# Seven-product gate/up blocks built inside PSUM, in a four-stage pipeline, with sums for the down stages on GpSimd

## The chip, the cores and the metric

One core of one Trainium2 chip. The metric is the device time of one execution in microseconds, as the median of several executions on the chip. Every execution lists its span by the profiler and the mean granted TensorE clock. All executions used here were of the fast state (the chip has a second, slower one) at a granted clock of 0.996 to 1.0. The time of an execution is longer than its span, and not by the same amount for both kernels: by 1.67 to 1.79 us in the 33 listed executions of the kernel before, by 1.77 to 3.14 us (median 2.15) in the 11 of the changed one. So spans are compared with spans and medians with medians.

## The reference, cut to what matters

Two blocks read the same 2048 x 640 input: a linear attention with 32 heads, and a GeGLU feed-forward with 1728 inner columns. A sigmoid gate mixes them. Inputs and output are bf16.

```python
q, k, v = split_heads(x @ wqkv)                   # 32 heads of 20
pq, pk = phi(q), phi(k)                           # phi(t) = where(t > 0, t + 1, exp(t)) + 1e-6
num = einsum("bhqd,bhde->bhqe", pq, einsum("bhsd,bhse->bhde", pk, v))
den = einsum("bhqd,bhd->bhq", pq, pk.sum over s)[..., None] + 1e-6
a = merge_heads(num / den) @ wo
b = (gelu(x @ w_gate) * (x @ w_up)) @ w_down
out = g * a + (1 - g) * b                         # g = sigmoid((x * gate_w).sum(-1))
```

## The kernel before

The 2048 rows are 16 positions of 128, in four row blocks (`q`) of 512. A row block has a **gate/up stage** (13 units of 128 inner columns, each `x @ w_gate` and `x @ w_up`, and one half unit) and a **down stage**. TensorE works through row block 0's gate/up, the K and G matrices of all positions, then gate/up 1, down 0, gate/up 2, down 1, gate/up 3, down 2, down 3.

A plain unit is ten matmuls of 512 columns. A **block** does the same by Strassen's scheme: it takes gate and up as the two rows of a 2 x 2 block matrix product and needs seven products of half the width in place of eight. For that it needs sums of weights (`ws`, later fetched from DRAM into `wr`) and of tokens (`tx`). The block before collects its parts in SBUF (`cg`, `ut`), and GpSimd makes the last product:

```python
    def phase_EW(q, ft, early, fetch):
        # ... x, ub, gb are PSUM banks, cg and ut SBUF tiles
        ew_mm(x[:, lo_h], 2, s_(2), t_(2), False, True)
        nc.scalar.copy(out=cg[:, hi_h], in_=x[:, lo_h])
        # ... four more products
        nc.vector.tensor_tensor(out=cg[:, hi_h], in0=ub[:, hi_h], in1=cg[:, hi_h], op=ALU.add)
        nc.scalar.activation(out=ut[:, 1], in_=x[:, lo_h], func=ACT.Copy, scale=HS)
        w_fetch(*fetch, eng=dma2)
        # ...
        nc.vector.tensor_tensor(out=cg, in0=gb, in1=cg, op=ALU.add)
        nc.vector.scalar_tensor_tensor(out=ut[:], in0=ub..., scalar=HS, in1=ut[:, 1:2]..., op0=ALU.mult, op1=ALU.add)
        # later: gelu on ScalarE, and hT = ut * gelu on GpSimd
```

The denominators of the attention are made for two positions at a time. GpSimd multiplies, VectorE reduces and inverts, GpSimd scales, and a transposing transfer brings the result into `pqT`.

```python
    def den_inv(st):
        for i in range(2):
            nc.vector.tensor_reduce(out=den[:, i, :], in_=dn[st + i]...)          # den <- prod
        nc.vector.scalar_tensor_tensor(out=dtmp[:], in0=den[:], scalar=EPS,       # two SBUF inputs
                                       in1=gsc["en"]..., op0=ALU.add, op1=ALU.mult)
        nc.vector.reciprocal(out=rg..., in_=dtmp[:])
```

The list `side` says which of this work is issued at which step of which stage. The down stages are Strassen products too; they need the **S sums** (`phase_S`, tiles `sw`, `s`, `sp`), which in this kernel VectorE makes, spread over the steps of the next gate/up stage.

Of the kernel before, what the change touches and what calls it, by code (L numbers as in the profile page):

```python
# [16 lines left out]
def kernel(  # L17
# [12 lines left out]
    nc = tc.nc  # L30
# [29 lines left out]
    def sums(out, a0, a1, op):  # L60
        nc.vector.tensor_tensor(out=out, in0=a0, in1=a1, op=op)
# [11 lines left out]
    held = set()  # L73

    def ps_tile(name, hold=False):
        b = bank_at[0] % NB
        while b in held:
            b = (b + 1) % NB
        bank_at[0] = b + 1
        if hold:  # L80
            held.add(b)
        return banks[:, b * QW : (b + 1) * QW]
# [8 lines left out]
    WF = tuple(range(4, 11))  # L91
    WS = 2 * 4 + 1
# [25 lines left out]
    def x_tiles():  # L118
        tx = big.tile([P, 4, 2, HT], FP16, name="tx", tag="pq", bufs=NQ)
        ew["tx"] = [tx[:, n] for n in range(4)]  # L120

    def cg_tile():
        ew["cg"] = big.tile([P, 2, QW], FP32, name="cg", tag="pq", bufs=NQ)

    x_tiles()
    cg_tile()
# [10 lines left out]

    ident = consts.tile([P, P], BF16, name="ident")
# [83 lines left out]
    def e_out(q, ft, psg, psu):  # L222
        gl = work.tile([P, QW], BF16, name="gl")
        nc.scalar.activation(out=gl[:], in_=psg[:], func=ACT.Gelu_apprx_tanh)  # L224
        nc.vector.scalar_tensor_tensor(out=hT_cur[q][:, ft, :], in0=psu[:], scalar=HS, in1=gl[:],  # L225
                                       op0=ALU.mult, op1=ALU.mult)

    def phase_E(q, ft, early=None):
        if ft < NF - 1:
            psg = ps_tile("ps_g")  # L230
            e_mm(psg, wg, ft, q)
            if early:
                early()
                ew_finish()
            psu = ps_tile("ps_u")
            e_mm(psu, wu, ft, q)
            e_out(q, ft, psg, psu)
        else:
            pgu = ps_tile("ps_gu")
            e_mm(pgu, wgu, 0, q)  # L240
            if early:
                early()
                ew_finish()
            gl = work.tile([P, QW], BF16, name="gl")
            nc.scalar.activation(out=gl[0:FL, :], in_=pgu[0:FL, :], func=ACT.Gelu_apprx_tanh)
            nc.vector.scalar_tensor_tensor(out=hT_cur[q][0:FL, ft, :], in0=pgu[FL:P, :], scalar=HS,
                                           in1=gl[0:FL, :], op0=ALU.mult, op1=ALU.mult)

    stash = dram.tile([len(WF), P, WS, P], FP16, name="stash")

    def w_sums(i):
        n = len(WF[2 * i : 2 * i + 2])
# [4 lines left out]
        for out, a0, a1, op in ((s1, u[:, :, 0:2, :], u[:, :, 2:4, :], ALU.add), (s2, s1, g[:, :, 0:2, :], ALU.subtract),  # L257
                                (s3, g[:, :, 0:2, :], u[:, :, 0:2, :], ALU.subtract),
                                (s4, g[:, :, 2:4, :], s2, ALU.subtract),
                                (o[:, 0:n, 8:9, :], g[:, :, 4:5, :], u[:, :, 4:5, :], ALU.subtract)):  # L260
# [18 lines left out]
    def ew_tiles():  # L279
        cg = ew["cg"]  # L280
        ew["cg"] = [cg[:, 0], cg[:, 1], zacc[:, 0:QW]]
        ew["n"] = 2
        ew["first"] = {}
        ew["open"] = []
        ew.setdefault("at", {})

    def w_fetch(*keys, eng=dma):
# [4 lines left out]
        for q, ft in keys:  # L292
            slot = ew["ring"][ew["m"] % 2]
            ew["m"] += 1
            eng(out=slot, in_=stash[WF.index(ft)])
            ew["at"][q, ft] = slot

    def ew_finish():
        for f in ew.get("open", ()):
            f()  # L300
        ew["open"] = []

    lo_h, hi_h = slice(0, HT), slice(HT, QW)

    def ew_mm(out, k, lhs, rhs, start=False, stop=False):
        for n in range(k):
            nc.tensor.matmul(out, lhsT=lhs(n), rhs=rhs(n), start=start and n == 0, stop=stop and n == k - 1,  # L307
                             skip_group_check=True)

    def ew_first(q, ft):  # L310
        x = ps_tile("ps_wx")
        cg = ew["cg"][ew["n"] % 3]
        ew["n"] += 1
        ew_mm(x[:, lo_h], 2, lambda n: wg[:, n, ft * P : (ft + 1) * P], lambda n: xT[q][:, n, lo_h], True, True)
        nc.scalar.copy(out=cg[:, lo_h], in_=x[:, lo_h])
        ew["first"][q, ft] = x, cg

    def phase_EW(q, ft, early, fetch):
        fs = slice(ft * P, (ft + 1) * P)
        sw_ = ew["at"][q, ft]  # L320
        if (q, ft) not in ew["first"]:
            ew_first(q, ft)
        x, cg = ew["first"][q, ft]

        def wt(w, k0):
            return lambda n: w[:, k0 + n, fs]

        def xt(k0, c):
            return lambda n: xT[q][:, k0 + n, c]

        def s_(i):
            return lambda n: sw_[:, 2 * (i - 1) + n, :]

        def t_(i):
            return lambda n: ew["tx"][i - 1][:, n, :]

        ub, gb = ps_tile("ps_wu"), ps_tile("ps_wg")
        ew_mm(ub, 1, wt(wu, 4), xt(4, slice(0, QW)), True)
        ew_mm(ub[:, lo_h], 2, wt(wu, 2), t_(4))
        ew_mm(gb[:, lo_h], 1, wt(wg, 4), xt(4, lo_h), True)  # L340
        ew_mm(gb[:, hi_h], 1, s_(5), xt(4, hi_h))
        ew_mm(x[:, lo_h], 2, s_(2), t_(2), False, True)
        nc.scalar.copy(out=cg[:, hi_h], in_=x[:, lo_h])
        early()
        ew_mm(gb[:, lo_h], 2, wt(wg, 2), xt(2, lo_h))
        ew_mm(ub[:, hi_h], 2, s_(1), t_(1), False, True)
        ew_mm(gb[:, hi_h], 2, s_(4), xt(2, hi_h), False, True)
        ew_mm(x[:, lo_h], 2, s_(3), t_(3), False, True)
        ut = work.tile([P, 2, HT], FP32, name="ut", tag="prod", bufs=2)
        nc.vector.tensor_tensor(out=cg[:, hi_h], in0=ub[:, hi_h], in1=cg[:, hi_h], op=ALU.add)  # L350
        nc.scalar.activation(out=ut[:, 1], in_=x[:, lo_h], func=ACT.Copy, scale=HS)  # L351
        w_fetch(*fetch, eng=dma2)
        ew_finish()
        nc.vector.tensor_tensor(out=cg, in0=gb, in1=cg, op=ALU.add)
        nc.vector.scalar_tensor_tensor(out=ut[:], in0=ub.rearrange("p (j c) -> p j c", j=2), scalar=HS,  # L355
                                       in1=ut[:, 1:2].to_broadcast([P, 2, HT]), op0=ALU.mult, op1=ALU.add)

        def finish():
            gl = work.tile([P, QW], BF16, name="gl")
            nc.scalar.activation(out=gl[:], in_=cg, func=ACT.Gelu_apprx_tanh)  # L360
            nc.gpsimd.tensor_tensor(out=hT_cur[q][:, ft, :], in0=ut[:].rearrange("p j c -> p (j c)"), in1=gl[:],  # L361
                                    op=ALU.mult)

        ew["open"].append(finish)
# [49 lines left out]
    def phase_KQ3(st):  # L414
# [3 lines left out]
        for lo, hi in CF:  # L418
            for dk in range(ND):
                kq_mm(ps[:, lo:hi], st, dk, lo, hi)  # L420
            top = min(hi, WQK - 1)
# [135 lines left out]
    zacc = consts.tile([P, D], FP32, name="zacc")  # L557
# [111 lines left out]
    def den_inv(st):  # L669
        den = work.tile([P, 2, H], FP32, name="den", bufs=2)  # L670
        for i in range(2):
            nc.vector.tensor_reduce(out=den[:, i, :], in_=dn[st + i][:].rearrange("p (h c) -> p h c", c=Dh),  # L672
                                    axis=AX.X, op=ALU.add)
        dtmp = work.tile([P, 2, H], FP32, name="dtmp", bufs=2)
        nc.vector.scalar_tensor_tensor(
            out=dtmp[:], in0=den[:], scalar=EPS, in1=gsc["en"][:, st : st + 2, None].to_broadcast([P, 2, H]),
# [4 lines left out]
        dn[st], dn[st + 1] = rg[:, 0], rg[:, 1]  # L681

# [36 lines left out]
    def phase_S(q, part, a=None, which=(3, 1, 2, 4)):  # L719
# [3 lines left out]
        def blk(i, k):  # L723
            return ktiles(part, k, hT_cur[q], pqT[q])[:, :, i * TW + c0 : i * TW + c1]

        s = {i: SS[q, i][:, lo:hi, c0:c1] for i in range(1, 5)}
        for i in which:
            a0, a1, op = {3: (blk(0, 0), blk(1, 0), ALU.subtract), 1: (blk(1, 0), blk(1, 1), ALU.add),
                          2: (s[1], blk(0, 0), ALU.subtract), 4: (blk(0, 1), s[2], ALU.subtract)}[i]
            sums(s[i], a0, a1, op)  # L730
# [12 lines left out]
    def phase_F(q):  # L743
# [34 lines left out]
        for a in range(2):  # L778
# [19 lines left out]
            product(x, a, 0, 0, 0, 0, 0, 0, True, True)  # L798
            c1 = keep("c1", x, 0)
# [32 lines left out]

    runs = {
        0: [3, -4, -5, 12, 13, -6, -7, 10, -8, 9, 11],
        1: list(range(1, NF)),
        2: [13, 0, 1, -4, -5, 2, -6, -7, 3, -8, -9, 12, -10, 11],
        3: [13, 0, 1, 2, -4, -5, 3, -6, -7, 12, -8, -9, 10, 11],
    }
    wins = [(q, -ft) for q in runs if q > 1 for ft in runs[q] if ft < 0]

    def next_fetch(q, ft):
        if (q, ft) not in wins:
            return ()
        k = wins.index((q, ft)) + 2
        return wins[k : k + 1]

    def run_E(q):
        for n, ft in enumerate(runs[q]):
            nxt = runs[q][n + 1] if n + 1 < len(runs[q]) else 0
            early = (lambda f=-nxt: ew_first(q, f)) if nxt < 0 else (lambda: None)  # L850
            if ft < 0:
                phase_EW(q, -ft, early, next_fetch(q, -ft))
            else:
                phase_E(q, ft, early if q != 1 else None)
            beside(q, n + (q == 1))
        ew_finish()

    with tc.manual_schedule(engines={mybir.EngineType.PE, mybir.EngineType.Activation, mybir.EngineType.DVE}):
# [9 lines left out]
    ew_tiles()  # L868
    side.update({
        (0, 0): [(w_sums, 1)],  # L870
        (0, 2): [(w_sums, 2)],
        (0, 8): [(x_sums, 3)],
# [3 lines left out]
    with tc.manual_schedule():  # L876
# [3 lines left out]
        w_sums(3)  # L880
# [25 lines left out]
    phase_E(1, 0)  # L906
    phase_KV()
    phase_Zrep()
# [20 lines left out]
    def m_part(i):  # L929
        phase_M(((0, 0), (0, 1), (1, 0)) if i == 0 else ((1, 1), (2, 0), (2, 1)))  # L930

    side.update({
        ("C", 0, 0): [(h_twin, 1)],
# [69 lines left out]
```

## Time and profile before

| | before |
|---|---|
| median of the runs given at the start (6) | 263.04 us |
| median of the 20 runs given with the result, these 6 among them | 262.23 us |
| median in the later sessions | 262.1 to 262.6 us |
| profiled span | 260.5 us |
| TensorE busy | 98% of the span |
| start of row block 0's gate/up | 21.8 us |
| gate/up of row block 0, 1, 2, 3 | 23.96, 31.77, 27.85, 27.96 us |
| K and G | 52.06 us |
| down stages 0 and 1 | 17.87 us each |

How to read it: TensorE is the bound from 12 us on, so a change is worth what it takes off TensorE's list, less the holes that it opens there. A stage's length is the distance between the first matmuls of two stages in TensorE's timeline. Row block 1's stage has further work in it besides its units, among it the products M, which join the attention's K-V sums with `wo`. The prediction below shows the lines that this rests on.

### The profile page before, as it was taken

The numbers are of one execution on the slowest core, as the hardware profiler recorded it, in microseconds if no ns is written. First come the engines' busy times: TensorE is split into PE (matmuls) and PEld (weight loads), VectorE is DVE, ScalarE is ACT, GpSimd is POOL, SyncE is SP. The second block draws the span as 40 slices with busy tenths as digits, with TensorE's granted clock in tenths as the row PEclk, the third lists the DMA queues.
The fourth block names the chain that finished last, engine by engine and source line by source line (L and its number), as shares of the span: only waits on it lengthen the run. The fifth ranks groups of instructions, "written<-read, shape, count | busy, mean of one in ns | idle before, by whom it ended". The sixth has DMA issues, their size and how long they took to land.

```text
span 260.5 us, 4715 instructions
## 1 busy us (share of the span) xinstructions
PE 255.3 (98%) x1713; PEld 156.7 (60%) x1713; DVE 203.6 (78%) x400; ACT 112.3 (43%) x241; POOL 106.4 (41%) x112
## 2 busy tenths in 40 slices
PE   7999999999999999999999999999999999999994
PEld 3554675555556775444476666757665775767672
DVE  0697667478779995699999969998789999777632
ACT  3689546655555233832231146654113665312110
POOL 6109896644551003685001875332892643000000
PEclk9999999999999999999999999999999999999999
DMA  6999999700000019125021258330123630011011
GB/s 222 280 300 306 205 321 276 302 4 0 0 0 3 0 21 334 42 69 112 9 93 52 50 107 150 104 113 1 53 50 101 143 92 0 3 50 47 6 50 50
DMA packets 37842, 26.84 MB, mean 103 GB/s; under 512 B 21052, under 2 KB 35260, under 8 KB 37820
## 3 DMA queue, kind: packets, MB, share of 16 engines
q1 hardware_dynamic: 35794, 22.81, 31.8%
q10 hardware_dynamic: 2026, 3.74, 5.5%
q8 instruction: 13, 0.21, 0.3%
q14 instruction: 9, 0.07, 0.1%
HBM read 16.45 MB, written 4.69 MB: 81 GB/s over the span
## 4 chain that ended last, share of the span: by engine, by line
PE 94%; DMA 4%; DVE 0%; SPq 0%; issue 0%
PE banks L219 30%; PE banks L764 26%; PE banks L405 15%; PE banks L307 14%; PE banks L503 6%; DMA wqk<-in_A_wqkv_dram 3%; PE banks L494 2%; DMA x_all<-in_A_x_dram 1%; PE banks L771 1%; PE banks L634 0%; PE banks L603 0%; DVE o_out L790 0%; SPq L155 0%; PE banks L573 0%
## 5 line engine op out<-in xcount | busy, mean ns | idle before, releaser
L224 ACT ACTIVATE gl<-banks 128x512 bf16<-128x512 f32 x34 | 20.2, 596 | 21.8 <-PE banks L219 18.6
L219 PEld LDWEIGHTS <-wu 128*128 128x128 bf16 x170 | 16.6, 98 | 18.2
L219 PEld LDWEIGHTS <-wg 128*128 128x128 bf16 x170 | 16.3, 98 | 16.9 <-issue 0.5
L422 ACT ACTIVATE phi<-banks 128x512 bf16<-128x512 f32 (+1 forms) x36 | 18.8, 526 | 16.3 <-POOL hold L737 8.9
L361 POOL TENSOR_TENSOR hT_151<-ut,gl 128x512 bf16<-128x512 f32 x12 | 15.0, 1260 | 14.6 <-ACT gl L360 11.0
L786 ACT ACTIVATE m_all<-banks,omg_s 128x320 f32<-128x320 f32 x16 | 8.4, 527 | 27.3 <-PE banks L764 27.2
L225 DVE SCALAR_TENSOR_TENSOR hb<-banks,gl 128x512 bf16<-128x512 f32 x20 | 13.4, 676 | 4.8 <-PE banks L219 2.6
L219 PE MATMUL banks<-xT_89,wg 128*128 128x512 bf16 x65 | 16.2, 379 | 0.0
L219 PE MATMUL banks<-xT_89,wu 128*128 128x512 bf16 x65 | 16.2, 379 | 0.0
L666 POOL TENSOR_TENSOR prod<-pq_95,zrep 128x640 f32<-128x640 bf16 x4 | 7.4, 1864 | 21.1 <-DVE den L672 21.1
L307 PE MATMUL banks<-tx,wr 128*128 128x256 f16 x78 | 14.9, 273 | 0.0
L790 DVE SCALAR_TENSOR_TENSOR o_out<-banks,omg_s,m_all 128x320 bf16<-128x320 f32 x24 | 12.0, 536 | 3.1 <-PE banks L764 3.1
L225 DVE SCALAR_TENSOR_TENSOR hT_151<-banks,gl 128x512 bf16<-128x512 f32 x14 | 9.6, 684 | 5.4 <-PE banks L219 2.4
L786 ACT ACTIVATE sw<-banks,omg_s 128x320 f32<-128x320 f32 x8 | 4.2, 528 | 21.0 <-PE banks L764 21.0
L405 PE MATMUL banks<-wqk,xT_88 128*128 128x512 bf16 (+2 forms) x80 | 12.3, 300 | 0.9 <-DMA wqk<-in_A_wqkv_dram 0.9
L355 DVE SCALAR_TENSOR_TENSOR ut<-banks,ut 128x512 f32<-128x512 f32 x18 | 12.3, 681 | 0.9 <-ACT ut L351 0.9
L424 DVE TENSOR_SCALAR phi<-phi 128x1280 bf16<-128x1280 bf16 x12 | 5.9, 492 | 8.8 <-ACT eneg L423 5.5
L307 PEld LDWEIGHTS <-wr 128*128 128x128 f16 x117 | 11.4, 98 | 1.5 <-DMA wr<-stash 0.2
L672 DVE TENSOR_REDUCE den<-prod 128x32 f32<-128x640 f32 x14 | 10.8, 810 | 0.9 <-POOL prod L666 0.9
L405 PE MATMUL banks<-wqk,xT_89 128*128 128x512 bf16 (+1 forms) x60 | 11.5, 344 | 0.0
L405 PE MATMUL banks<-wqk,xT_91 128*128 128x512 bf16 (+1 forms) x60 | 11.5, 344 | 0.0
L405 PE MATMUL banks<-wqk,xT_90 128*128 128x512 bf16 (+1 forms) x60 | 11.5, 344 | 0.0
(278 smaller groups left out, 645.1 us busy)
## 6 DMA issues: line engine op xcount, KB each, us to landing
wr<-stash ACTq DMA_DIRECT2D x11, 288.0 KB, 2.8
out_dram<-o_out SPq DMA_DIRECT2D x16, 160.0 KB, 1.7
wd<-in_B_w_down_dram SPq DMA_DIRECT2D x1, 2080.0 KB
x_all<-in_A_x_dram SPq DMA_DIRECT2D x3, 640.0 KB, 4.8
wqk<-in_A_wqkv_dram SPq DMA_DIRECT2D x1, 800.0 KB
wg<-in_B_w_gate_dram SPq DMA_DIRECT2D x1, 800.0 KB
wu<-in_B_w_up_dram SPq DMA_DIRECT2D x1, 800.0 KB
wv<-in_A_wqkv_dram SPq DMA_DIRECT2D x1, 800.0 KB
```

The costliest lines, as they stand in the source:

```text
L219: nc.tensor.matmul(ps[:, t0 : t0 + tw], lhsT=w[:, dk, ft * P : (ft + 1) * P], rhs=xT[q][:, dk, t0 : t0 + tw], start=(dk == 0), stop=(dk == ...
L224: nc.scalar.activation(out=gl[:], in_=psg[:], func=ACT.Gelu_apprx_tanh)
L225: nc.vector.scalar_tensor_tensor(out=hT_cur[q][:, ft, :], in0=psu[:], scalar=HS, in1=gl[:], op0=ALU.mult, op1=ALU.mult)
L307: nc.tensor.matmul(out, lhsT=lhs(n), rhs=rhs(n), start=start and n == 0, stop=stop and n == k - 1, skip_group_check=True)
L355: nc.vector.scalar_tensor_tensor(out=ut[:], in0=ub.rearrange("p (j c) -> p j c", j=2), scalar=HS, in1=ut[:, 1:2].to_broadcast([P, 2, HT]), ...
L361: nc.gpsimd.tensor_tensor(out=hT_cur[q][:, ft, :], in0=ut[:].rearrange("p j c -> p (j c)"), in1=gl[:], op=ALU.mult)
L405: nc.tensor.matmul(ps[:, 0 : hi - lo], lhsT=xT[q][:, dk, sl * P : (sl + 1) * P], rhs=wqk[:, dk, lo:hi], start=(dk == 0), stop=(dk == ND - 1),)
L422: nc.scalar.activation(out=e[:, lo:top], in_=ps[:, lo:top], func=ACT.Exp)
L503: nc.tensor.matmul(bank[:, 0:HALF], lhsT=lhsT, rhs=rhs, start=(start and n == 0), stop=(stop and n == NG2 - 1), skip_group_check=True)
L764: nc.tensor.matmul(bank[:, 0:HALF], lhsT=lhs(sa, ia, ka * KS + kk, a), rhs=rhs(sb, kb * KS + kk, jb), start=(start and kk == 0), stop=(sto ...
L786: nc.scalar.activation(out=c[:], in_=bank[:, 0:HALF], func=ACT.Copy, scale=omg[i])
L790: nc.vector.scalar_tensor_tensor(out=out, in0=bank[:, 0:HALF], scalar=omg[i], in1=c[:], op0=ALU.mult, op1=ALU.add)
```

## The change

The intent: 28 blocks in place of 18. For that a block must need less of the other engines. It is now built inside PSUM, the memory that matmuls write to (eight banks here, `GB` and `UB` in the diff): ScalarE copies a half bank into another bank, VectorE adds into a bank, and matmuls go on adding to what they wrote. Four stages of consecutive blocks are interleaved on TensorE so that these steps lie beside other blocks' products. A plain unit ("filler") is put beside the first two steps, when the pipeline is not yet full (the **ramp**; the steps that empty it are the **drain**). VectorE gets `hT` back from GpSimd. GpSimd gets the S sums of row blocks 1 and 2. There are four fetch buffers in place of two, and the fetches move from ScalarE's queue to SyncE's.

```diff
+    GB, UB = (0, 1, 2), (3, 4, 5, 6, 7)
...
+        def p1():
+            two(ub[:, lo_h], wg[:, 0:2, fs], X[:, 0:2, lo_h])
+            nc.scalar.copy(out=gb[:, lo_h], in_=ub[:, lo_h])
+            nc.scalar.copy(out=cp, in_=ub[:, hi_h])
+        def p6():
+            two(ub[:, lo_h], s_(2), tx[1])
+            nc.vector.tensor_tensor(out=gb[:, hi_h], in0=ub[:, lo_h], in1=cp, op=ALU.add)
+        def p7():
+            two(ub[:, lo_h], s_(3), tx[2])
+            nc.scalar.copy(out=c3, in_=ub[:, lo_h])
+        def p3():
+            nc.vector.tensor_tensor(out=ub[:, hi_h], in0=ub[:, hi_h], in1=c3, op=ALU.add)
+            two(gb[:, hi_h], s_(4), X[:, 2:4, hi_h])
+            w_fetch(*fetch)
...
+        return [p5, p1], [p6], [p7, p3, g5, p2], [u5, p4]
...
-        2: [13, 0, 1, -4, -5, 2, -6, -7, 3, -8, -9, 12, -10, 11],
-        3: [13, 0, 1, 2, -4, -5, 3, -6, -7, 12, -8, -9, 10, 11],
+        2: blocks([NF - 1, 1, 12], 0, range(2, 12), [None]),
+        3: blocks([1, 12], 0, range(2, 12), [NF - 1]),
...
+                nxt = runs[q][n + 1] if n + 1 < len(runs[q]) else 0
+                new = unit(q, ft, GB, (1, 3)) if isinstance(nxt, tuple) else unit(q, ft)
...
+                    plain[f] = unit(q, f, GB, (1, 2))
...
+            for f in s0[:1] + s2[:2] + s0[1:2] + s1 + extra + s2[2:] + s3 + s0[2:]:
...
-        (2, 0): [(cg_tile,), (ew_tiles,), (s_tiles, 1), (den_mul, 8, 9)],
-        (2, 1): [(den_inv, 8), (den_out, 8, 9)],
+        (2, 0): [(ring_more,), (w_fetch, (2, 4), (2, 5)), (s_tiles, 1), (den_mul, 8, 9), *s_pool(1, 0)],
+        (2, 5): [(den_sum, 8, 0)],
+        (2, 6): [(den_sum, 8, 1)],
+        (2, 7): [(den_rec, 8)],
+        (2, 9): [(den_out, 8, 9), *s_pool(1, 1)],
...
-        (3, 0): [(t_sums, 3), (s_tiles, 2)],
-        (3, 1): [(den_inv, 14), (den_out, 14, 15)],
+        (3, 0): [(s_tiles, 2), (den_inv, 14), *s_pool(2, 0)],
+        (3, 8): [(den_out, 14, 15), *s_pool(2, 1)],
```

`s_pool(q, a)` is `phase_S` for all three parts on GpSimd.

## The prediction

> **What bounds the kernel now.** I read the page first: busy shares, then the chain that ended last.
>
> ```profile
> span 260.5 us, 4715 instructions
> PE 255.3 (98%) x1713; PEld 156.7 (60%) x1713; DVE 203.6 (78%) x400; ACT 112.3 (43%) x241; POOL 106.4 (41%) x112
> ...
> PE 94%; DMA 4%; DVE 0%; SPq 0%; issue 0%
> ```
>
> A busy PE can still be waiting inside modelled matmuls, so the second view is PE's own waits. It holds two lines, both from the first 12 us:
>
> ```profile
> PE banks L405 <- DMA wqk<-in_A_wqkv_dram: 0.9, 2, 0.5
> PE banks L185 <- PEq L987: 0.8, 1, 0.8
> ```
>
> From 12.0 to 257.0 us the chain in order of time is TensorE alone. It also gives the price of a unit (chain pieces: start, us, what):
>
> ```profile
> 199.78 0.22 PE banks L307 x2
> 200.00 1.08 PE banks L219 x5
> 201.08 3.71 PE banks L307 x32
> ```
>
> L219 is a plain unit's half: 5 matmuls of 512 columns, 1.08 us, so 0.2158 us each and 2.158 us a unit. L307 is the seven-product block: two blocks are 34 matmuls in 0.22 + 3.71 = 3.93 us. At 0.1087 us per 256 columns the ideal is 1.955 us a block. A block therefore saves 0.20 us over a plain unit, and nothing that does not shorten TensorE's list, or open a hole in it, can move the end.
>
> **Holes that are there already.** I set each gate/up stage of the timeline against counts times durations. Row block 0 (21.90 to 45.88, with one earlier plain unit): 6 x 2.158 + 1.08 + 5 x 1.955 = 23.80, took 23.98. Row block 2: 27.71, took 27.85. Row block 3: 27.92, took 27.97. Together 0.37 us. There is little waste to recover.
>
> **What the Trainium skill says.** "TensorE: Matmul & The Clock Gate", section "Wait — 56ns, not 53.3ns?": columns over 2.4 GHz plus about 2.5 ns per matmul. The trace agrees: 215.8 ns for 512 columns, 108.7 for 256; so a matmul count matters far less than columns. "PSUM — Partial Sum Buffer", section "The four PSUM rules": VectorE and ScalarE writes don't change the bits that decide whether a matmul adds, and a matmul without the first flag adds to what they wrote where the bit is set. The new block is built on this; the trace before has no such write and cannot confirm it. Same page, "PSUM bank collisions raise a hardware error": two engines must not be in one bank at once. That is why the new block's steps on a bank form a strict chain TensorE, ScalarE or VectorE, TensorE. "SBUF — State Buffer", section "🔬 SBUF: two separate sides": a VectorE instruction with two SBUF inputs and a GpSimd one lock each other out for a whole instruction. The trace agrees:
>
> ```profile
> 166.99 0.28 DVE L61 TENSOR_TENSOR s_1_1694<-pqT_1594 128x256 f16<-128x256 bf16 x1
> 167.19 0.41 DVE L350 TENSOR_TENSOR cg<-banks,cg 128x256 f32<-128x256 f32 x1
> ...
> 170.63 1.13 DVE L61 TENSOR_TENSOR s_2_1695<-s_1_1694,pqT_1594 128x256 f16<-128x256 f16 x1
> ```
>
> The same 256-element S sum took 0.28 us with GpSimd idle and 1.13 beside its product. An instruction with one PSUM input isn't caught: 0.41 us at 155.48 too, in the middle of GpSimd work.
>
> **Part 1, the blocks' arithmetic.** Blocks go from 18 (5, 7, 6 in row blocks 0, 2, 3) to 28 (8, 10, 10). The new block has 14 matmuls of 256 columns and two of 512, because gate's fifth K tile becomes one matmul: 14 x 0.1087 + 2 x 0.2158 = 1.953 us. Ten more blocks save 10 x 0.205 = 2.05 us. If the pipelining were perfect the old holes would go too: 0.37 more, so 260.6 us at best.
>
> **Part 2, the other engines in a block.** Before, per block: VectorE 0.42 + 0.69 + 0.68, ScalarE three copies and a gelu, GpSimd one 1.16 to 1.3 us product. After: VectorE two 256-column adds (0.42 each) and one 0.69 product; cadence about 1.33 us of the 1.95. ScalarE three copies (0.27 apart) and a gelu (0.52): 1.33 us. Neither is the bound. GpSimd leaves hT and gets the S sums of row blocks 1 and 2: at 1.12 us per 512 elements, four sums of 768, 256 and 128 elements are about 10.8 us per half. With two products (2.8) and two scalings (2.5), row block 2 gives it 27 us beside 27 us of TensorE. The second half is wanted only some 11 us into the following down stage, so it should fit. The extra weight sums (20 x 1.12 = 22.4 us from 20 us on) keep ahead of a block every 1.95 us.
>
> **Part 3, the new holes.** I walked the four-stage order with the trace's delays: TensorE's last column to ScalarE 0.20 us, to VectorE 0.26, back to TensorE about 0.07. The tight link is the sixth product: add on VectorE into the gate bank, then the seventh product on the same up bank at the next step. In steady state the add ends about 1.77 us into the step and is wanted at 2.17, so it holds. It does not where steps are short or VectorE has something else:
> - ramp: the step without the last stage is 0.43 us shorter, a hole of 0.2 us, three times: 0.6;
> - drain of row block 2, which ends in two empty steps: 0.2;
> - row block 2's two den reductions and the reciprocal pair, now between blocks:
>
> ```profile
> 153.35 0.82 DVE L672 TENSOR_REDUCE den<-prod 128x32 f32<-128x640 f32 x1 [0.55 <-POOL prod L666]
> 154.21 0.23 DVE L675 SCALAR_TENSOR_TENSOR dtmp<-den,en_s 128x64 f32<-128x64 f32 x1
> 154.46 0.55 DVE L680 RECIPROCAL rg<-dtmp 128x64 f32<-128x64 f32 x1
> ```
>
>   about 0.77 us each on a VectorE with 0.6 spare per step: holes of 0.3, 0.15 and 0.15, plus 0.2 if the two-input instruction meets GpSimd: 0.8 together;
> - row block 1, where the changed loop runs the up matmuls one step late. The instruction order shows six PSUM banks for M between a gate product and the next gate into the bank that its gelu still reads. M lasts 0.53 us; gelu is done 0.8 after the gate:
>
> ```profile
> 102.58 0.60 ACT L224 ACTIVATE gl<-banks 128x512 bf16<-128x512 f32 x1 [0.46 <-PE banks L219]
> ```
>
>   (its gate's last matmul was issued by 102.38). A hole of 0.25 us, twice: 0.5.
> Sum of new holes: 0.6 + 0.2 + 0.8 + 0.5 = 2.1 us, nearly the whole gain. Walked strictly: 263.04 - 2.05 - 0.37 + 2.1 = 262.7.
>
> **The rivals.** (a) *The holes stay hidden.* TensorE has more slack than I give it, since its waits are set only against the actual end of the other engine and my 0.07 is one observation. For it: the steady state has 0.4 us to spare and the den work was visibly split up to fit. Then about 260.6 to 261.2. (b) *Weight fetches become the wait.* A slot is refilled after its block's fourth sum product and wanted two steps later: 3.9 - 0.85 = 3.05 us.
>
> ```profile
> wr<-stash ACTq DMA_DIRECT2D x11, 288.0 KB, 2.8
> ```
>
> It is 256 KB now, so just in time, on a queue that also holds transposes. If landing took 3.5 us, six fetches in each of two stages would cost 0.2 to 0.3 each: 264 to 265. Against it: the transposes sit behind the last urgent fetch. (c) *GpSimd becomes the bound*, if its sums run at twice the isolated time: 10 us late into the down stages of row blocks 1 and 2, 266 or more. Against it: VectorE has almost no two-SBUF-input work during the blocks.
>
> **The number.** The strict walk says 262.7, rival (a) 260.9; I don't know which slack is real and take 262.0. The range 260.5 to 264.0 runs from all holes hidden to rival (b). Faster by over 2% would need 257.8, below the arithmetic's floor of 260.6: 1%. Slower by over 2% (268.3) needs rival (c) or a stall at every step: 2%.
>
> **What would show it.** Block stages of the changed trace: row block 0, with its earlier unit and the two postponed u5/p4 products, near 23.4 us; row block 2 near 28.3 (27.1 without holes), row block 3 near 27.3. In the waits, TensorE on VectorE and on ScalarE, each under 0.5 us, at ramps, beside den and around M; the down stages unchanged at 17.9 us. VectorE's adds into PSUM at 0.42 us; GpSimd's sums at about 1.7 us per 768 elements. It would be wrong if a hole recurs at every step (VectorE or ScalarE slower into PSUM than out of it), if TensorE waits for the fetched weights, or if a down stage grows because an S sum is late.

## The result, and the profile after

The changed kernel took 264.09 us in the median (262.78 to 266.14, 10 runs), the kernel before 262.23 (261.36 to 263.55, 20 runs). The ratio of the fast runs is **1.0068**, with a 95% interval of 1.0043 to 1.0093. A ratio is the mean time of one kernel's fast runs over that of the other's of the same rounds, so it isn't quite the ratio of these medians. The results are correct, which confirms for this case that matmuls go on adding to what ScalarE and VectorE wrote into a bank. The change made the kernel slower by 0.7%, where 0.4% faster was predicted. The time lies 0.1 us above the range.

First the page after: the span and busy shares, and the chain's shares by engine.

```profile
span 261.7 us, 4830 instructions
...
PE 254.2 (97%) x1755; PEld 160.8 (61%) x1755; DVE 189.4 (72%) x372; ACT 121.9 (47%) x271; POOL 130.4 (50%) x142
...
PE 89%; DMA 5%; DVE 2%; issue 1%; POOL 1%; ACT 0%; SPq 0%; POOLq 0%; DVEq 0%; ACTq 0%
```

TensorE's busy time fell from 255.3 to 254.2 us, yet the span grew. VectorE is now 2% of the chain that ended last, where it had been 0%. The waits of TensorE after (what it waited for: us in all, times, longest us) say where:

```profile
PE banks L320 <- DVE hb L246: 1.2, 1, 1.2
PE banks L311 <- DMA wr<-stash: 0.9, 1, 0.9
...
PE banks L320 <- ACT gl L241: 0.4, 2, 0.2
```

None of these was there before. The stages, measured in the same way, with two of the experiments beside them. Matmuls that a stage leaves over for the next are counted with their own stage (0.43 us), and a missing matmul record at a stage's border is put back (0.2 us):

| us | before | after | hold (e1) | three edits (e8) |
|---|---|---|---|---|
| start of row block 0 | 21.76 | 21.35 | 21.09 | 21.49 |
| gate/up 0 | 23.96 | 23.34 | 23.35 | 23.34 |
| K and G | 52.06 | 52.06 | 52.06 | 52.07 |
| gate/up 1 | 31.77 | 32.25 | 32.25 | 31.77 |
| down 0 | 17.87 | 17.87 | 17.87 | 17.87 |
| gate/up 2 | 27.85 | 29.04 | 28.08 | 27.67 |
| down 1 | 17.87 | 17.87 | 17.86 | 17.87 |
| gate/up 3 | 27.96 | 28.66 | 27.44 | 27.31 |
| span | 260.5 | 261.7 | 259.2 | 258.8 |

The start hangs on the first loads and varies from execution to execution: the three edits of e8 don't touch it, and e5, with two of them, started row block 0 at 21.91 us. Down stages and K and G didn't change.

**The longest hole, in row block 3.** TensorE's timeline after (start, us, engine, line, operation, counts, and in brackets the idle time before and its releaser):

```profile
200.04 0.38 PE L311 MATMUL banks<-tx,wr_1721 128*128 128x256 f16 x2
201.66 1.24 PE L320 MATMUL banks<-xT_91,wu 128*128 128x512 bf16 x5 [1.23 <-DVE hb L246]
```

Two matmuls of 256 columns issued at 200.04 are through in 0.22 us, at 200.26. The next starts at 201.66: a hole of 1.40 us. VectorE's timeline of the same stretch:

```profile
197.25 1.53 DVE L699 TENSOR_REDUCE den<-prod 128x32 f32<-128x640 f32 x2
198.82 1.65 DVE L704 SCALAR_TENSOR_TENSOR dtmp<-den,en_s 128x64 f32<-128x64 f32 x1
200.50 0.55 DVE L709 RECIPROCAL rg<-dtmp 128x64 f32<-128x64 f32 x1
200.97 0.63 DVE L246 SCALAR_TENSOR_TENSOR hb<-banks,gl 128x512 bf16<-128x512 f32 x1
```

and GpSimd's:

```profile
197.16 1.64 POOL L61 TENSOR_TENSOR sw<-hT_152 128x768 f16<-128x768 bf16 x1
198.76 1.63 POOL L61 TENSOR_TENSOR s_1_2270<-hT_152 128x768 f16<-128x768 bf16 x1
200.47 1.64 POOL L61 TENSOR_TENSOR s_2_2271<-s_1_2270,hT_152 128x768 f16<-128x768 f16 x1
```

GpSimd's second sum starts at 198.76. VectorE's `dtmp`, 64 elements with both inputs in SBUF, starts at 198.82 and ends at 200.47, when that sum is over and the third one starts. So it lasts 1.65 us. The `hb` product behind it reads the PSUM bank that the filler unit's up half is to use, and TensorE starts 0.69 us after that product did. In the kernel before, VectorE made the same inversion in the same stage, 7.2 us after its start (here it is 5.0):

```profile
200.35 0.23 DVE L675 SCALAR_TENSOR_TENSOR dtmp<-den,en_s 128x64 f32<-128x64 f32 x1
200.61 0.55 DVE L680 RECIPROCAL rg<-dtmp 128x64 f32<-128x64 f32 x1
```

0.23 us. GpSimd's timeline there has nothing between the scaling at 194.06 and the next one, which waits for this very reciprocal:

```profile
194.06 2.68 POOL L689 TENSOR_TENSOR pq_615<-pq_615,rg 128x640 bf16<-128x640 bf16 x2
201.31 2.50 POOL L689 TENSOR_TENSOR pq_615<-pq_615,rg 128x640 bf16<-128x640 bf16 x2 [4.57 <-DVE rg L680]
```

**The other holes after.** In row block 1, TensorE waits twice for a gelu on ScalarE whose bank it wants back, 0.15 and 0.21 us. In row block 2 it waits for fetched weights, at two places: 0.26 us at the first fetch into the second pair of buffers (155.5 us), and 1.08 us at 169.5 us. The second one in TensorE's timeline, and SyncE's queue before it:

```profile
170.56 0.39 PE L311 MATMUL banks<-tx,wr 128*128 128x256 f16 x2 [0.92 <-DMA wr<-stash]
```

```profile
164.33 2.39 SPq L305 DMA_DIRECT2D wr<-stash  x2
166.77 3.28 SPq L724 DMA_TRANSPOSE pqT_1942<-pq_630  x2
```

The fetch that TensorE waits for had just been issued when two transposes followed on the queue.

### The profile page after: what moved, and what is told of

Read it like the earlier page. It is cut to its first block, busy times and chain, and to the rows that moved or that the text cites.

```text
span 261.7 us, 4830 instructions
## 1 busy us (share of the span) xinstructions
PE 254.2 (97%) x1755; PEld 160.8 (61%) x1755; DVE 189.4 (72%) x372; ACT 121.9 (47%) x271; POOL 130.4 (50%) x142
## 3 DMA queue, kind: packets, MB, share of 16 engines
HBM read 17.86 MB, written 5.24 MB: 88 GB/s over the span
## 4 chain that ended last, share of the span: by engine, by line
PE 89%; DMA 5%; DVE 2%; issue 1%; POOL 1%; ACT 0%; SPq 0%; POOLq 0%; DVEq 0%; ACTq 0%
PE banks L798 26%; PE banks L311 19%; PE banks L430 16%; PE banks L320 15%; PE banks L529 6%; PE banks L236 3%; DMA wqk<-in_A_wqkv_dram 2%; PE banks L520 2%; DMA wr<-stash 2%; PE banks L805 1%; DMA pqT_1615<-pq_93 1%; DMA wr_1721<-stash 1%; DVE dtmp L704 1%; DVE den L699 1%; DVE hb L246 1%
## 5 line engine op out<-in xcount | busy, mean ns | idle before, releaser
L241 ACT ACTIVATE gl<-banks 128x512 bf16<-128x512 f32 x52 | 30.9, 597 | 31.2 <-PE banks L320 25.1
L246 DVE SCALAR_TENSOR_TENSOR hb<-banks,gl 128x512 bf16<-128x512 f32 x26 | 17.7, 683 | 10.9 <-PE banks L320 6.5
L246 DVE SCALAR_TENSOR_TENSOR hT_152<-banks,gl 128x512 bf16<-128x512 f32 x26 | 17.9, 689 | 9.3 <-PE banks L311 4.3
L320 PEld LDWEIGHTS <-wu 128*128 128x128 bf16 x100 | 9.8, 98 | 11.9 <-issue 1.4
L320 PEld LDWEIGHTS <-wg 128*128 128x128 bf16 x100 | 9.8, 98 | 11.7 <-issue 0.4
L371 DVE TENSOR_TENSOR banks<-banks,zacc 128x256 f32<-128x256 f32 x28 | 12.1, 430 | 6.7 <-ACT zacc L368 4.8
L311 PEld LDWEIGHTS <-wg 128*128 128x128 bf16 x140 | 13.7, 98 | 4.6
L368 ACT COPY zacc<-banks 128x256 f32<-128x256 f32 x28 | 10.4, 371 | 10.9 <-PE banks L311 10.8
L824 DVE SCALAR_TENSOR_TENSOR m_all<-banks,omg_s,m_all 128x320 f32<-128x320 f32 x8 | 4.4, 548 | 13.2 <-PE banks L798 13.2
L430 PE MATMUL banks<-wqk,xT_89 128*128 128x512 bf16 (+1 forms) x60 | 11.7, 344 | 0.0
L311 PE MATMUL banks<-tx,wr_1721 128*128 128x256 f16 x60 | 11.5, 273 | 0.1
```

The costliest lines, as they stand in the source:

```text
L241: nc.scalar.activation(out=gl[:], in_=psg[:], func=ACT.Gelu_apprx_tanh)
L246: nc.vector.scalar_tensor_tensor(out=hT_cur[q][:, ft, :], in0=psu[:], scalar=HS, in1=gl[:], op0=ALU.mult, op1=ALU.mult)
L311: nc.tensor.matmul(out, lhsT=lhsT, rhs=rhs, start=start, stop=True, skip_group_check=True)
L320: return lambda: nc.tensor.matmul(ps, lhsT=w[:, k, f * P : (f + 1) * P], rhs=xT[q][:, k, :], start=(k == 0), stop=(k == ND - 1))
L368: nc.scalar.copy(out=c3, in_=ub[:, lo_h])
L371: nc.vector.tensor_tensor(out=ub[:, hi_h], in0=ub[:, hi_h], in1=c3, op=ALU.add)
```

## The experiments

The theory, **lock**: the S sums that were moved to GpSimd run back to back where VectorE makes the inversion of positions 14 and 15. Its two-input instruction is locked out for a whole sum, and the late product passes this on to TensorE through a PSUM bank. Rivals: the **bank** order of the filler unit is at fault whatever VectorE does; the **fetches** are late because of the transposes behind them (theory T) or because of SyncE's queue (theory Q); the S sums' **place** on GpSimd is worth its price after all. Ten kernels ran, each with 5 rounds. Every ratio is to the kernel before on the same chip.

### e0: the changed kernel again

No edit; the control.

> The changed kernel unaltered, as the yardstick of this chip session. All theories: some 1.5 to 2 us slower than the kernel before (ratio near 1.007), row block 3's gate/up stage near 28.7 us of TensorE against 28.0 before, row block 2's near 29.0 against 27.85. If the two large holes of the first profile (1.1 us behind a weight fetch, 1.4 us behind VectorE's locked two-input instruction) are chance events of one execution, this profile shows them smaller or elsewhere.

Measured: 263.70 us, ratio 1.0057 (1.0023 to 1.0090). The 1.4 us hole is there again (1.39, `dtmp` 1.65), and so are the gelu waits. The 1.08 us fetch hole isn't there; the first-fetch hole is 0.43. What follows: the lock hole belongs to the kernel, the 1.08 one to some executions. The spans of the six runs go from 260.6 to 263.2.

### e1: GpSimd held until the reciprocals are there

```diff
-        (3, 0): [(s_tiles, 2), (den_inv, 14), *s_pool(2, 0)],
+        (3, 0): [(s_tiles, 2), (den_inv, 14), (lambda: pool_hold(dn[14][:, 0, :]),), *s_pool(2, 0)],
```

`pool_hold` is a one-element copy on GpSimd that reads the reciprocal.

> GpSimd's S sums of row block 2 wait until VectorE has finished the last reciprocal pair (one GpSimd hold). Theory L (lock): the two-SBUF-input instruction falls from 1.65 to 0.22 us, the 1.4 us hole at row block 3's ramp goes to 0 to 0.2, the stage takes 27.3 us, the kernel is 1.2 us faster than the changed kernel. Rival B (VectorE's den work itself, 2.3 us in the ramp, is too long whatever GpSimd does): a hole of 0.8 or more remains. Rival C (late S sums): moving GpSimd's work 3 us later makes the down stage of row block 2 grow from 17.9 us.

Measured: 261.67 us, ratio **0.9974** (0.9952 to 0.9996). VectorE and GpSimd in its timeline:

```profile
197.61 0.23 DVE L704 SCALAR_TENSOR_TENSOR dtmp<-den,en_s 128x64 f32<-128x64 f32 x1
```

```profile
198.49 0.18 POOL L771 COPY hold<-rg 128x1 f32<-128x1 f32 x1 [2.51 <-DVE rg L709]
198.62 1.64 POOL L61 TENSOR_TENSOR sw<-hT 128x768 f16<-128x768 bf16 x1
```

`dtmp` is back at 0.23 us, and TensorE no longer waits for VectorE at all. Row block 3 took 27.44 us in place of 28.66, the down stages are unchanged. One instruction of 0.18 us is worth 2.0 us in the medians (263.70 to 261.67). In the fastest spans of the six runs of each it is 1.4 us (260.6 to 259.2), which is the hole's size; the rest of the 2.0 is the slow tail of e0's runs, which this kernel didn't show. The lock theory holds.

### e2: the filler's up half in another bank

```diff
-                    plain[f] = unit(q, f, GB, (1, 2))
+                    plain[f] = unit(q, f, UB, (1, 3))
```

> The plain unit that fills the ramp writes its up half to a bank of the up ring instead of the gate-ring bank that the plain unit before it used; nothing else moves. Theory L says the lock delays VectorE and the shared bank passes the delay on: with another bank TensorE goes on, and only the first add into the gate bank is late, so the hole at row block 3's ramp falls from 1.4 to about 0.5 us; the two-input instruction still takes 1.65 us. If the hole stays at 1.2 to 1.4, the bank had no part in it.

Measured: 262.73 us, ratio 1.0017 (0.9992 to 1.0043). `dtmp` still takes 1.64 us, but the hole is 0.43 in place of 1.40, and TensorE's wait is now for the next thing that VectorE does late, its add into PSUM:

```profile
PE banks L311 <- DVE banks L364: 0.3, 1, 0.3
```

Row block 3 took 27.69 us. The bank decides how much of VectorE's delay reaches TensorE; the delay itself is the lock's. Both halves of the mechanism are seen apart.

### e3: the transposes of positions 8 and 9 in the down stage

```diff
-        (2, 9): [(den_out, 8, 9), *s_pool(1, 1)],
+        (2, 9): s_pool(1, 1),
+        ("F", 1, 0): [(den_out, 8, 9)],
```

> The scaling and the two transposes of row block 2 (positions 8, 9) move from the tenth step of the gate/up stage to the down stage after it, behind the second S-sum half; the weight fetches are then alone on the queue. Theory T (the transposes slow the fetch issued 0.4 us before them): the 1.1 us wait for fetched weights goes, landing stays at 2.5 to 3.0 us for every fetch, row block 2's stage takes 27.9 us, the kernel is 1 us faster than the changed kernel. Rival F (the fetch is late by its own latency, or by chance): a wait of 0.3 us or more for fetched weights remains somewhere in the stage.

Measured: 264.10 us, ratio 1.0066 (1.0044 to 1.0087). The 1.08 us fetch hole isn't there, but the control hadn't shown it either, so this says nothing about theory T. What came instead wasn't expected: a hole of 1.02 us in the middle of row block 2. Positions 8 and 9's `dtmp`, which takes 0.21 us in the changed kernel, and GpSimd beside it:

```profile
164.87 1.13 DVE L704 SCALAR_TENSOR_TENSOR dtmp<-den,en_s 128x64 f32<-128x64 f32 x1
```

```profile
164.28 1.64 POOL L61 TENSOR_TENSOR sw<-hb 128x768 f16<-128x768 bf16 x1
```

In the changed kernel GpSimd's scaling waits for this reciprocal, so GpSimd is idle while `dtmp` runs. With the scaling moved away the next S sums start at once and lock it out. It is the lock a second time, made by accident at another place.

### e4: the hold, and the first fetch on ScalarE's queue

```diff
-        (2, 0): [(ring_more,), (w_fetch, (2, 4), (2, 5)), ...
+        (2, 0): [(ring_more,), (lambda: w_fetch((2, 4), (2, 5), eng=dma2),), ...
```

> The GpSimd hold of the earlier run (e1) plus one change: the two weight fetches at the head of row block 2's gate/up stage are issued from ScalarE's DMA queue instead of SyncE's, where they stand behind transposes that wait for GpSimd's scaling. Theory Q (queue order makes the first fetch late): the 0.4 us hole before row block 2's third block (0.38 to 0.62 in four profiles) goes, the stage falls by 0.4 us, the kernel is 0.3 to 0.4 us faster than e1. Rival (the fetch itself is too slow): the hole stays.

Measured: 262.54 us, ratio 1.0020 (0.9984 to 1.0055), so 0.5% slower than e1 against before. It was run at another time. The first-fetch hole did not go, it grew to 1.30 us, and TensorE now waits for ScalarE. TensorE's line, then ScalarE's queue and work (ACTq is its instruction stream):

```profile
155.30 0.38 PE L311 MATMUL banks<-tx,wr 128*128 128x256 f16 x2 [1.14 <-ACT zacc L360]
```

```profile
153.02 0.85 ACTq L305 DMA_DIRECT2D wr<-stash  x2
153.97 0.60 ACT L241 ACTIVATE gl<-banks 128x512 bf16<-128x512 f32 x1 [4.36 <-PE banks L320]
154.60 0.36 ACT L359 COPY banks<-banks 128x256 f32<-128x256 f32 x1
```

Theory Q fell. The fetch isn't held back by what is ahead of it on SyncE's queue. It starts at 153.02 here and at 153.07 in e1, where it is on SyncE's queue (the stage starts at 146.65 and 146.62). The buffer that it writes had held `pq` of positions 4 to 7, and the transposes of positions 6 and 7 must have read it first. On ScalarE's stream that wait holds up the gelu and the copies behind it: in e1 the same gelu starts at 151.19. (The view puts the 4.36 us down to TensorE, but the gate matmuls of this gelu were through by 151.0.)

### e5: the hold, and row block 1 in the plain order

```diff
+        if q == 1:
+            for n, ft in enumerate(runs[1]):
+                phase_E(1, ft)
+                beside(1, n + 1)
+            return
         pipe, plain, at = [], {}, []
```

(and the hold of e1)

> The GpSimd hold of e1 plus row block 1 issued as in the kernel before (gate then up of one unit, no late up half). The prediction's step: the late up half cost 0.5 us there, two waits on ScalarE's gelu around the M matmuls (31.77 before, 32.24 after). If right, row block 1's stage returns to 31.8 us, TensorE's 0.4 us wait on gelu goes, the kernel is 0.5 us faster than e1. If the stage stays at 32.2, the cause is elsewhere.

Measured: 261.18 us, ratio 0.9959 (0.9929 to 0.9989). Both gelu waits are gone and row block 1 took 31.77 us, as before. That is the predicted 0.5 us, shown by taking it back. Its profile has a first-fetch hole of 0.72 us.

### e6: the S sums back on VectorE

```diff
-        (2, 0): [..., (den_mul, 8, 9), *s_pool(1, 0)],
+        (2, 0): [..., (den_mul, 8, 9)],
...
-        (3, 0): [(s_tiles, 2), (den_inv, 14), *s_pool(2, 0)],
-        (3, 8): [(den_out, 14, 15), *s_pool(2, 1)],
+        (3, 0): [(s_tiles, 2), (den_inv, 14)],
+        (3, 8): [(den_out, 14, 15)],
+        ("F", 1, 0): [(phase_S, 1, "h", 1), (phase_S, 1, "p", 1), (phase_S, 1, "x", 1)],
...
+    for q in (1, 2):
+        for k, work_ in ((3, ("h", 0, (3,))), (4, ("h", 0, (1,))), (8, ("h", 0, (2,))), ...):
+            side.setdefault((q + 1, k), []).append((phase_S, q, *work_))
```

No hold; the `phase_S` work of row blocks 1 and 2 is spread over VectorE's steps 3, 4 and 8 to 12 of the next gate/up stage and the start of the down stage, much as in the kernel before.

> The changed kernel with the S sums of row blocks 1 and 2 back on VectorE, spread over the gate/up steps as before. Theory L: the two-input instruction at row block 3's ramp runs at 0.22 us and the 1.4 us hole goes, since GpSimd is idle there. VectorE then has 0.5 to 0.65 us sums where 0.6 us a step is spare: holes of 0.1 to 0.3 us at some seven steps in each of two stages, 1.5 to 3 us in all. So about 0.5 us faster to 1.5 us slower than the changed kernel. If it is faster by 1 us or more, moving the sums to GpSimd was itself the loss.

Measured: 262.63 us, ratio 1.0015 (0.9983 to 1.0047). `dtmp` takes 0.23 us, row block 3 takes 27.26 us, and there is a new hole of 0.56 us at the end of row block 2, where VectorE's add is late behind its sums:

```profile
PE banks L311 <- DVE banks L364: 0.4, 1, 0.4
```

The 1.5 to 3 us of holes that were expected here, at some seven steps in each of two stages, didn't come. The median is 1.1 us below that of e0, where 0.5 had been the most expected and 1 us or more was the mark for calling the move itself a loss. So moving the sums to GpSimd without a hold cost about 0.4% (1.0057 against 1.0015; the intervals overlap); with the hold it is at least no worse than this (0.9974 against 1.0015). They were run at other times. The sums on VectorE together with the edits of e5 and e8 were not run. This profile's granted clock was 0.996.

### e7: hold, plain order and the other queue together

The edits of e4 and e5 in one kernel:

```diff
-        (2, 0): [(ring_more,), (w_fetch, (2, 4), (2, 5)), ...
+        (2, 0): [(ring_more,), (lambda: w_fetch((2, 4), (2, 5), eng=dma2),), ...
-        (3, 0): [(s_tiles, 2), (den_inv, 14), *s_pool(2, 0)],
+        (3, 0): [(s_tiles, 2), (den_inv, 14), (lambda: pool_hold(dn[14][:, 0, :]),), *s_pool(2, 0)],
+        if q == 1:                       # in run_E: row block 1 by phase_E, as in e5
```

> The hold, the fetch on the other queue and row block 1's old order together. If the three are independent: 0.8 to 0.9 us below e1, so some 1.6 us below the kernel before (ratio 0.993 to 0.995). What is left then is the ramps, the den work of row block 2 and its drain, together under 1 us; the arithmetic's floor is 2.05 us under the kernel before.

Measured: 262.48 us, ratio 1.0002 (0.9972 to 1.0032). A miss: the edit of e4 brings its hole along (1.26 us at 154.1, the same wait on ScalarE), and outweighs the gain of e5, which is there (row block 1 took 31.77 us).

### e8 and e9: the first fetch earlier, and its control

e9 is e5 again. e8 is e5 with the token sums moved behind the inversion:

```diff
-        ("F", 0, 1): [(h_twin, 1), (x_tiles,), (t_sums, 2), (den_inv, 4), (den_mul, 6, 7), (den_out, 4, 5)],
+        ("F", 0, 1): [(h_twin, 1), (den_inv, 4), (den_mul, 6, 7), (den_out, 4, 5)],
...
-        (2, 0): [(ring_more,), (w_fetch, (2, 4), (2, 5)), (s_tiles, 1), (den_mul, 8, 9), ...
+        (2, 0): [(x_tiles,), (t_sums, 2), (ring_more,), (w_fetch, (2, 4), (2, 5)), (s_tiles, 1),
+                 (lambda: pool_hold(ew["tx"][3][:, 0, 0:1]),), (den_mul, 8, 9), ...
```

> The hold and the plain order of row block 1 as in the best run so far, and besides the four token sums of row block 2 go from VectorE's list ahead of the reduction of positions 4 and 5 to the list of the first step of row block 2, so that the reduction starts at 139.2 us in place of 140.7 and GpSimd and the transposes of positions 6 and 7 are done about 1.6 us sooner. Theory (the hole of 0.4 to 0.7 us before the third unit of row block 2 is the fetch that waits until those transposes have read its buffer): the hole goes, TensorE's list stays as it is, and the kernel runs 0.3 to 0.6 us faster than the same kernel without this edit: ratio to before 0.993 to 0.995 where that one shows 0.996. Rival 1 (the fetch itself is slow, by contention with the transposes on the queue): the hole stays at 0.4 or more. Rival 2 (the sums collide with GpSimd, or delay the plain unit's product on VectorE): a hole at VectorE appears between 149 and 154 us, and the ratio stays at 0.996 or rises.

> The best run so far again (GpSimd held until the reciprocals of positions 14 and 15, row block 1 in the plain order), as the control of the other run of this call: ratio to before 0.995 to 0.997, a hole of 0.4 to 0.7 us at the first fetch into the second pair of buffers, row block 1's gate/up stage at 31.8 us.

Measured: e8 **260.86** us, ratio **0.9946** (0.9917 to 0.9974); e9 261.42 us, ratio 0.9984 (0.9951 to 1.0017). The fetch on SyncE's queue and the matmuls that need it, in e9:

```profile
153.66 0.80 SPq L305 DMA_DIRECT2D wr<-stash  x2
```

```profile
156.29 0.61 PE L311 MATMUL banks<-tx,wr 128*128 128x256 f16 x4 [0.41 <-DMA wr<-stash]
```

and in e8:

```profile
151.46 0.80 SPq L305 DMA_DIRECT2D wr<-stash  x2
```

```profile
155.19 0.60 PE L311 MATMUL banks<-tx,wr 128*128 128x256 f16 x4
```

The fetch starts 2.2 us sooner, 1.7 us counted from the start of the stage (147.07 us in e9, 146.54 in e8), and TensorE doesn't wait. A part of this is again the lock: positions 6 and 7's `dtmp` meets GpSimd in e9 (0.92 us) and no longer in e8 (0.22). Row block 2 took 27.67 us, the shortest of all runs, with no wait on VectorE between 149 and 154 us. The first-fetch hole is the buffer's late release, as expected; both rivals fell. (e8 alone could not tell the buffer from the queue, on which everything came earlier too; e4 had ruled out the queue.) In the medians the step is worth 0.56 us, as expected; the intervals of the two ratios overlap, and their larger distance comes from e9's runs. Two of its six have spans of 261.1 us, the other four 259.2 to 259.8, and the profiled one of the slow two has the hole of the first profile again:

```profile
PE banks L311 <- DMA wr<-stash: 1.4, 2, 1.0
```

(1.13 us at 170.0, behind the transposes of positions 8 and 9, and 0.58 at the first fetch). **This one stays open.** It was seen in two profiles, of the changed kernel and of e9, in which the fetch of that moment was issued right before those transposes; other profiles with the same order on the queue (e0, e5) don't show it, nor does e8's profile, and the spans of e8's six runs (258.1 to 259.6) leave no room for it. Why the fetch lands late in some executions only, no run here tells.

e8 beats both kernels: 0.5% faster than the kernel before, 1.1 to 1.2% faster than the changed one by the ratios (0.9946 against 1.0057 and 1.0068). They were run at other times.

## Why the prediction was wrong, point by point

- **What bounds it, the price of a unit, the blocks' saving: right.** Row block 0 was predicted at about 23.4 us and took 23.34. Without the lock, row block 3 took 27.26 to 27.51 against a predicted 27.3. The down stages stayed at 17.87, predicted 17.9. Of the 2.4 us that the arithmetic allowed, e8 got 1.4 by the medians of its call (262.27 to 260.86) and 1.7 by the spans of the profiles.
- **The other engines in a block: right.** VectorE's adds into PSUM took 0.42 to 0.43 us, GpSimd's 768-element sums 1.64 (predicted 1.7). Half of the S sums of a row block took 11.2 us (152.89 to 164.08); the 10.8 of part 2 doesn't follow from its own 1.12 us per 512 elements, which give 10.1. No hole recurs at every step. Rival (c), GpSimd as the bound, didn't come: no down stage grew.
- **The failing step is the lock in part 3 and in rival (c).** The prediction quoted the lock and measured its size, then gave it 0.2 us, "plus 0.2 if the two-input instruction meets GpSimd", in row block 2 only, and dismissed it for the blocks because "VectorE has almost no two-SBUF-input work during the blocks". One such instruction was enough. In row block 2 it was harmless (0.21 us), as GpSimd waited for its result, and by luck: the first half of the S sums had ended only 0.2 us before (164.08, `dtmp` at 164.27). In row block 3 it opened 1.40 us. The row `(3, 0)` of the diff has the inversion and the S sums side by side; the step that was missing was to lay GpSimd's new list beside each `dtmp`. Even before, `dtmp` took 0.81 to 1.03 us where it met GpSimd in the down stages, so the size could have been read there. (The two lines that the prediction compares are different sums; but `s_2` too takes 0.29 us where GpSimd is idle.) That the lock is the cause is shown by e1 (lock removed) and e3 (made anew); e2 (the same delay, let through less) shows the path to TensorE.
- **Row block 1: right.** 0.48 us for 0.5, through the named wait, and e5 took it back.
- **Ramp, drain and den: too large.** Ramps 0.11 us each at three places in place of 0.2; the drain of row block 2 0.12 for 0.2; its den holes 0.28 for 0.8. Together 0.73 us where 1.6 was put.
- **Rival (b), the fetches: half right, for another reason.** It put the wait at the refill of a slot, in every stage. What came was one at the first use of the second pair of buffers, 0.26 to 0.72 us, because a transposing transfer must read that buffer first (e4 and e8), and one of about 1.1 us in some executions, whose cause is open.
- **The choice of the number: wrong.** The strict walk said 262.7, and the prediction went down to 262.0 on the hope that holes stay hidden. Its upper end, 264.0, was also only the lower end of what it gave rival (b), 264 to 265. With the measured holes the walk gives - 2.05 - 0.37 + 0.73 + 0.48 + 1.40 + 0.26 = + 0.45 us, and + 1.53 with the fetch wait of 1.08. The profiled span of the changed kernel, which has that wait, is 1.2 us longer, with a start that was 0.4 us earlier: so the walk accounts for the span. The mis-sized term was the lock: 1.40 us against 0.2 at another place.
- **What stays open.** The medians of the same runs differ by 1.86 us (262.23, 264.09). Some 0.4 us of this lies in the part of the time that is outside the span (1.7 us before, 2.15 after, in the median; 1.77 to 3.14 us in the 11 listed executions of the changed kernel), which the prediction didn't consider and no run here explains. The base was luck too: 263.04 is the median of six runs and stands 0.8 us above that of the 20.

## What to carry to other kernels

When work moves to GpSimd, go through every VectorE instruction with two SBUF inputs that will run beside it. Each can last as long as the GpSimd instruction that it meets, however small it is itself, and it counts in full where a PSUM bank behind it is wanted soon. A one-element copy on GpSimd that reads VectorE's result puts the two in order and cost 0.18 us here. And when a buffer is to be filled early, look for the last reader of its former content: moving that reader forward helped, while another queue only moved the wait onto an engine that had work to do.

## What the Trainium skill lacked or had wrong

- "SBUF — State Buffer", section "🔬 SBUF: two separate sides", has the lock right: `dtmp` ended when the GpSimd sum that had started 0.06 us before it ended. What it lacks is a number for a tiny instruction: 0.23 us alone, 1.65 beside sums of 1.64, 1.13 when the sum had already run for 0.6.
- "Perfetto Trace Analysis", section "Summary: the profiler window per engine type", lists what the reported window of a VectorE instruction hides, but doesn't say where a lock shows. Here it's inside the reported duration (1.65 us, busy), so no wait and no idle time of VectorE points to it.
- "GPSIMD Engine Reference", section "3.1 Elementwise — side-by-side cycle accounting", gives a two-input add as 1.96 times slower than on VectorE, for 2048 fp32 elements. With bf16 and fp16 operands the runs show more: 1.64 us against 0.56 for 768 elements (2.9 times) and 0.67 against 0.28 for 256 (2.4 times).
- No page that was read gives the cost of a transfer issued from ScalarE while its buffer is not yet free. It held up that engine's later gelu and copies: a hole of 1.30 us on TensorE in e4, 1.26 in e7. It belongs to "Perfetto Trace Analysis", section "DMA Instruction — HWDGE (DVE, Sync)", whose timeline has the wait in the issuing sequencer.
